# Turning the inputs of the second mixture by block transposes on VectorE and DMAs through DRAM instead of TensorE's transposes

## The chip, the cores and the metric

The kernel runs on one core of a Trainium2 chip. The metric is device microseconds of one execution. Engines are named as the profile names them: PE (TensorE, matrix products and transposes), PEld (its weight loads), DVE (VectorE), ACT (ScalarE), POOL (GpSimd) and SP (SyncE, which here issues every DMA).

## What is computed

Three stages follow each other: an attention with pooled queries, a first mixture with a gate, and a second mixture. The change is in the second one:

```python
def _moe2_ref(x, w_theta, w_tok_r, w_tok_i, w_ch):      # x: 4 x 576 x 512
    theta = x @ w_theta
    cos_t, sin_t = (np.cos(theta), np.sin(theta))
    zr = x * cos_t
    zi = x * sin_t
    y = einsum('ts,bsd->btd', w_tok_r, zr) + einsum('ts,bsd->btd', w_tok_i, zi)
    u = x + y
    return u + np.maximum(u @ w_ch, 0.0)
```

All of it is float32. The kernel computes each product as three products of float32r halves (`PASS`), a high and a low part of both operands.

## The kernel before

The first mixture leaves x transposed: `XT[b]` holds, for batch b, the 512 features on 4 x 128 partitions and the 576 tokens along the columns. The second mixture needs x both ways. `theta(n)` takes features on partitions (a block of 128 tokens of `XT` as the stationary operand); the products `x * cos` and `x * sin` need the same 128 tokens on partitions, because theta comes out of TensorE that way.

There are 18 blocks, `angles`: five for the even batches (four of 128 tokens and one that holds the last 64 tokens of two batches), four for the odd ones. For each block n:

- `turn(n)` makes the token-major copy: four TensorE transposes into PSUM bank 6 (L1042), and two ScalarE copies (L1045) into the tiles `yt[n, 0]` and `yt[n, 1]`, whose tags are t0 and t1 for even n, t2 and t3 for odd n.
- `ysplit(n)` cuts the feature-major block into its high and low part (ScalarE, and POOL at L1033).
- `theta(n)` makes twelve products (L1084), then VectorE reduces the angle (`near`, L1090 to L1092; `rest`, L1095 and L1096; `clip`, L1099), ScalarE makes sine and cosine (`wave`), and `mult` multiplies them by `yt` (L1114: the first on VectorE, the second on POOL; for the shared blocks `tails`, L1074 and L1075), and `zcut` cuts the result in two (L1065, L1066).

`mix(b, c0)` then mixes the tokens (L1138): nine parts of twelve products, one part for each piece of the token weights `WTK[j]`. `final(b, c0)` makes the product with `w_ch` (L1157) and stores the output.

What sets the order is a count of ticks. Each part of a product of TensorE ends with `tick()`; `after(k, f)` puts f k ticks ahead. `theta(n)` ends with `prepare(n + 1)`, which puts `turn(n + 1)` at TURN ticks and `ysplit(n + 1)` at YS ticks; `rest`, `clip`, `wave` and `mult` come at 1, 2, 4 and 5 ticks (`THETA`). Each engine works through its own list in the order in which it was written.

Around the seam of the two mixtures the order is hidden(6), theta(0), value(6), theta(1), hidden(7), theta(2), the first half of value(7), theta(3), the rest of value(7), theta(4), mix(0, 0). `hidden` (L841) and `value` (L860) are products of the first mixture. Between theta(4) and mix(0, 0) stand the DMA loads of the token weights: nine of 576 KB (L1180), into the buffers of value(7)'s weights, so that all but the first wait for a part of value(7); behind them four loads of w_ch (L1183).

Of the kernel before, what the change touches and what calls it, by code (L numbers as in the profile page):

```python
# [11 lines left out]
F32 = mybir.dt.float32  # L12
# [3 lines left out]
ALU = mybir.AluOpType  # L16
# [12 lines left out]
HALF = 288  # L29
# [1 line left out]
THIRDS = 6  # L31
AHEAD = 3
SHIFT = 24
TURN = 4
TPOS = ((1, 0), (1, 3), (2, 0), (3, 0), (3, 3))
THETA = (1, 2, 4, 5)
YM = (1, 0)
# [25 lines left out]
def attn_moe_kernel(ctx: ExitStack, tc: tile.TileContext, qT, kT, vP, muk, mur, wk, wv, wr, wth, wtr, wti, wch, ident, out):  # L63
    nc = tc.nc
    pe, act, dve, pool, sp = nc.tensor, nc.scalar, nc.vector, nc.gpsimd, nc.sync
# [3 lines left out]
    dram = ctx.enter_context(tc.tile_pool(name="dram", bufs=2, space=DRAM))  # L69

    idn = const.tile([128, 128], F32, name="idn")
# [9 lines left out]
    XT = [big.tile([128, 4, 577 + 63 * (1 - b % 2)], F32, name=f"xt{b}") for b in range(NB)]  # L81
# [630 lines left out]
    def mixtures(WR, nat, cp):  # L712
# [4 lines left out]
        def mem_tile(shape, dt, tag):  # L717
            return (early if tag in EARLY_TAGS else mem).tile(shape, dt, tag=tag, name=tag)
# [9 lines left out]
        def psum_at(i):  # L728
            return (psm + psn)[i]()
# [9 lines left out]
        def tile_x(i):  # L739
            return mem_tile([128, 576], F32R, f"x{i}")  # L740

        def tile_g(i):
            return mem_tile([128, 1152], F32, f"g{i}")
# [8 lines left out]
        def tile_q(i):  # L752
            return mem_tile([128, 1024], F32R, f"q{i}")

        def pair(t):
            return t.rearrange("p (a b) -> p a b", a=2)
# [5 lines left out]
        def after(n, fn, *args):  # L762
            queue.setdefault(now[0] + n, []).append((fn, args))

        def tick():
            now[0] += 1
            for fn, args in queue.pop(now[0], []):
                fn(*args)
# [116 lines left out]
        for k in range(4):  # L885
            x = pair(ready[k // 2][:, 576 * (k % 2):576 * (k % 2) + 576])
# [33 lines left out]
        t = now[0] + 1.0  # L920
# [116 lines left out]
        def turn(n):  # L1037

            b, i = angles[n]
            ps = psum_at(6)  # L1040
            for k in range(4):
                pe.transpose(ps[:, 128 * k:128 * k + 128], XT[b][:, k, 128 * i:128 * i + 128], idn)  # L1042
            for a in range(2):
                yt[n, a] = mem_tile([128, HALF], F32, f"t{2 * (n % 2) + a}")
                act.copy(yt[n, a][:, 0:256], ps[:, 256 * a:256 * a + 256])  # L1045

        yt = {}

        def prepare(n):
            if n < len(angles):  # L1050
                after(TURN, turn, n)
                if n:
                    after(YS, ysplit, n)
# [3 lines left out]
        def zcut(j, z):  # L1057
            assert cnt.get(j, 2) == 2
            cnt[j] = 0
            if j == 9:  # L1060
                zs[j] = [tile_x(4 - Y0 + a)[:, 0:DM] for a in range(2)]
            else:
                t = tile_a(zroom[j])
                zs[j] = [t[:, 0:DM], t[:, DM:2 * DM]]
            act.copy(zs[j][0], z)  # L1065
            pool.tensor_tensor(zs[j][1], z, zs[j][0].bitcast(F32), ALU.subtract)  # L1066

        def tails(yn, q, r):
            for o in range(2):
                z = tile_x(6 - Y0 + o)[:, 0:DM].bitcast(F32)  # L1070
                c = slice(64 * o, 64 * o + 64)
                for a, y in enumerate(yn):
                    w = slice(256 * a, 256 * a + 256)
                    dve.tensor_tensor(z[0:64, w], y[c, 0:256], q[c, w], ALU.mult)  # L1074
                    dve.tensor_tensor(z[64:128, w], y[c, 0:256], r[c, w], ALU.mult)  # L1075
                zcut(8 + o, z)

        def theta(n):
            b, i = angles[n]
            y = ys.pop(n)  # L1080
            ps = psum_at(4)
            for k in range(4):
                for p, (x, w) in enumerate(PASS):
                    pe.matmul(ps, lhsT=y[k // 2][:, k % 2, x], rhs=WT[k][:, w], start=(k == 0 and p == 0), stop=(k == 3 and p == 2))  # L1084
            tick()
            qr = tile_q(n % 2).bitcast(F32)
            q, r = qr[:, 0:DM], qr[:, DM:2 * DM]

            def near():
                dve.tensor_scalar(q, ps, float(np.float32(1 / (2 * math.pi))), MAGIC, op0=ALU.mult, op1=ALU.add)  # L1090
                dve.tensor_scalar(q, q, -MAGIC, 1.0, op0=ALU.add, op1=ALU.mult)
                dve.scalar_tensor_tensor(out=r, in0=q, scalar=-C1, in1=ps, op0=ALU.mult, op1=ALU.add)  # L1092

            def rest():
                dve.scalar_tensor_tensor(out=r, in0=q, scalar=-C2, in1=r, op0=ALU.mult, op1=ALU.add)  # L1095
                dve.scalar_tensor_tensor(out=r, in0=q, scalar=-C3, in1=r, op0=ALU.mult, op1=ALU.add)  # L1096

            def clip():
                dve.tensor_scalar(r, r, PI_LO, -PI_LO, op0=ALU.min, op1=ALU.max)  # L1099

            def wave():
                act.activation(q, r, AF.Abs)  # L1102
                act.activation(r, r, AF.Sin)
                act.activation(q, q, AF.Sin, scale=-1.0, bias=hpi)

            def mult():
                yn = [yt.pop((n, a)) for a in range(2)]
                if i == 4:
                    tails(yn, q, r)
                    return  # L1110
                for j, t in ((i, q), (4 + i, r)):
                    for a in range(2):
                        w = slice(256 * a, 256 * a + 256)
                        (dve, pool)[YM[j // 4]].tensor_tensor(t[:, w], yn[a][:, 0:256], t[:, w], ALU.mult)  # L1114
                    zcut(j, t)

            near()
            for t, f in zip(THETA, (rest, clip, wave, mult)):
                if t:
                    after(t, f)  # L1120
                else:
                    f()
            prepare(n + 1)
            tick()
# [59 lines left out]
        n = 5  # L1184
# [61 lines left out]
```

## Time and profile before

| | us |
|---|---|
| median of 3 runs | 917.83 |
| lowest and highest | 917.63, 918.45 |
| the profiled execution | 917.41 |
| span of the profiled execution | 915.6 |
| its second mixture, first L1042 to the end | 643.9 to 915.6 |

The span is the time from the first to the last instruction that the profile shows; the time of an execution is 1.8 us longer here. The second mixture shares its start with the last two blocks of the first one. The rows of the trace on which the prediction rests stand in a section of their own below; a row of a timeline gives the start, the length, the engine, the line, the operation with its tiles (out <- in), a count of merged instructions, and in brackets the idle time ahead of it and what ended that.

### The profile page before, as it was taken

To read this page: it belongs to the slowest core of one execution; us is meant where nothing else is said; L and a number is where in the kernel's file an instruction comes from. 1 tells how busy PE (TensorE), PEld (TensorE's weight loads), DVE (VectorE), ACT (ScalarE), POOL (GpSimd) and SP (SyncE) were. 2 spreads that over 40 slices of the span, in tenths; PEclk is the share of its full clock that TensorE was granted. 3 is DMA by queue.
4 is the path that set the end of the run, shared out by engine and by line. 5 is a ranking of instruction groups with operands and counts; after the bars stand their busy time and mean duration, and the time that the engine had idled before them with its cause. 6 is when DMAs were issued, how large, how long until landed. Compare 5 with 4: busy or idle time off the path is not lost.

```text
span 915.6 us, 17370 instructions
## 1 busy us (share of the span) xinstructions
PE 902.5 (99%) x6292; PEld 783.0 (86%) x6292; DVE 689.0 (75%) x965; ACT 540.2 (59%) x1131; POOL 594.8 (65%) x660
## 2 busy tenths in 40 slices
PE   8999999999999999999899999999999999999998
PEld 6777777777777777777889999999999999999998
DVE  7988888888988888882689888888758563676712
ACT  7777777777777777764665655555354442443410
POOL 7877777777787777764386566656567574665631
PEclk9999999999999999999999999999999999999999
DMA  7567877776777886659503333333508000010001
GB/s 225 170 183 218 241 222 191 214 216 206 216 209 211 241 229 188 176 154 346 224 12 116 100 99 104 96 98 113 187 2 273 27 28 26 1 53 1 27 26 52
DMA packets 59157, 130.92 MB, mean 143 GB/s; under 512 B 10816, under 2 KB 29952, under 8 KB 59072
## 3 DMA queue, kind: packets, MB, share of 16 engines
q1 hardware_dynamic: 59072, 129.82, 47.6%
q8 instruction: 49, 0.80, 0.4%
q14 instruction: 36, 0.29, 0.1%
HBM read 70.46 MB, written 22.17 MB: 101 GB/s over the span
## 4 chain that ended last, share of the span: by engine, by line
PE 91%; POOL 3%; DMA 2%; ACT 1%; issue 1%; DVE 1%; SPq 0%; ACTq 0%; DVEq 0%; POOLq 0%
PE sc L310 18%; PE ty L430 16%; PE ps L1138 13%; PE ps L860 11%; PE ps L841 10%; PE ps L1157 6%; PE ps L1084 5%; PE ty L396 4%; PE ps L810 3%; PE tx L396 3%; DMA b<-wv 2%; PE sc L396 2%; PE ps L1042 1%; POOL q L201 1%; POOL kt L201 1%
## 5 line engine op out<-in xcount | busy, mean ns | idle before, releaser
L331 DVE TENSOR_REDUCE m<-sc 128x1 f32<-128x1152 f32 x138 | 185.8, 1347 | 46.3 <-PE sc L310 45.6
L343 ACT ACTIVATE e<-sc,m 128x1152 f32<-128x1152 f32 x144 | 176.4, 1225 | 60.9 <-DVE m L331 56.3
L310 PE MATMUL sc<-kt,q 128*128 128x384 f32 (+1 forms) x864 | 192.1, 351 | 1.6 <-ACT E L407 1.0
L310 PEld LDWEIGHTS sc<-kt,q 128*128 128x128 f32 (+1 forms) x864 | 146.8, 190 | 22.4 <-issue 13.8
L1138 PE MATMUL ps<-b,a 128*128 128x288 f32 x816 | 111.2, 295 | 0.0
L1138 PEld LDWEIGHTS ps<-b,a 128*128 128x128 f32 x816 | 109.3, 188 | 0.6
L841 PE MATMUL ps<-x,a 128*128 128x288 f32 x768 | 105.3, 298 | 2.5 <-ACT g L823 2.4
L841 PEld LDWEIGHTS ps<-x,a 128*128 128x128 f32 x768 | 103.8, 191 | 3.0 <-ACT g L823 2.6
L860 PE MATMUL ps<-k,b 128*128 128x288 f32 x768 | 103.5, 295 | 0.0
L860 PEld LDWEIGHTS ps<-k,b 128*128 128x128 f32 x768 | 102.1, 188 | 0.3
L201 POOL TENSOR_TENSOR kt<-kn,kh 64x576 fp32r<-64x576 f32 (+1 forms) x64 | 87.5, 1387 | 2.4
L363 DVE STREAM_TRANSPOSE blk<-e 128x1152 f32<-128x1152 f32 x60 | 81.6, 1360 | 7.5 <-ACT e L343 7.5
L430 PE MATMUL ty<-M,vn 128*64 128x320 f32 x576 | 84.4, 438 | 0.2 <-ACT M L407 0.2
L430 PEld LDWEIGHTS ty<-M,vn 128*64 128x64 f32 x576 | 38.7, 136 | 36.3 <-issue 3.8
L476 POOL TENSOR_TENSOR xt<-xt,rb 128x576 f32<-128x576 f32 x16 | 21.9, 1370 | 73.0 <-ACT xt L440 73.0
L828 POOL TENSOR_TENSOR k<-h,k 128x288 fp32r<-128x288 f32 x64 | 59.1, 939 | 15.1 <-ACT k L827 14.9
L430 PE MATMUL ty<-E,vn 128*64 128x256 f32 x540 | 64.9, 385 | 0.0
L844 DVE TENSOR_TENSOR h<-h 128x288 f32<-128x288 f32 x64 | 42.3, 663 | 22.3 <-ACT h L843 21.6
L1102 ACT ACTIVATE q<-q 128x512 f32<-128x512 f32 x18 | 11.4, 632 | 77.2 <-DVE q L1099 77.2
L810 PE MATMUL ps<-x,blk 128*128 128x288 f32 x384 | 54.3, 301 | 2.1 <-POOL x L790 1.9
L407 DVE COPY M<-tx 128x512 f32<-128x512 f32 x80 | 54.5, 681 | 1.8 <-PE tx L396 1.8
L430 PEld LDWEIGHTS ty<-E,vn 128*64 128x64 f32 x540 | 36.1, 136 | 22.8 <-issue 7.6
(147 smaller groups left out, 1753.3 us busy)
## 6 DMA issues: line engine op xcount, KB each, us to landing
E<-blk SPq DMA_DIRECT2D x240, 144.0 KB
vn<-vP SPq DMA_DIRECT2D x16, 576.0 KB
kn<-kT SPq DMA_DIRECT2D x15, 576.0 KB
qn<-qT SPq DMA_DIRECT2D x15, 576.0 KB
b<-wtk SPq DMA_DIRECT2D x9, 576.0 KB
rb<-scr SPq DMA_DIRECT2D x32, 144.0 KB
out<-xt SPq DMA_DIRECT2D x32, 144.0 KB
cv<-wk SPq DMA_DIRECT2D x8, 512.0 KB
```

What stands on the lines that cost most here:

```text
L201: engines[e].tensor_tensor(out, x, hi.bitcast(F32), ALU.subtract)
L310: r = pe.matmul(sc[0:m, c, 0:384], lhsT=x, rhs=k[:, 384 * c:384 * c + 384], start=(i == 0), stop=(i == len(ops) - 1),)
L331: r = dve.tensor_reduce(m, scs[n][:, :, 0:384], axis=AX.XY, op=ALU.max, negate=True)
L343: r = act.activation(e, sc[:, :, 0:384], AF.Exp, bias=m, scale=1.0, accum_out=rss[P][:, t:t + 1])
L363: dve.transpose(out, es_[n].rearrange("p a b -> p (a b)").rearrange("p (k m i) -> p k m i", k=KT, m=4))
L396: r = pe.transpose(ps[:, 128 * j:128 * j + 128], flat[:, 128 * k:128 * k + 128], idn)
L430: pe.matmul(out, lhsT=vns[P][:, h, j], rhs=e, start=(x == 0), stop=(x == KT - 1))
L810: pe.matmul(pss[d], lhsT=WR[k][:, w, 128 * d:128 * d + 128], rhs=x[k][:, c], start=(k == 0 and n == 0), stop=(k == 3 and n == 2))
L828: pool.tensor_tensor(q[:, 1], h, q[:, 0].bitcast(F32), ALU.subtract)
L841: pe.matmul(ps, lhsT=WK[k, f // 4][:, w, 128 * (f % 4):128 * (f % 4) + 128], rhs=x[k][:, c], start=(k == 0 and n == 0), stop=(k == 3 and n ...
L860: pe.matmul(pss[d], lhsT=WV[f][:, w, 128 * d:128 * d + 128], rhs=k2[f][:, c], start=(f == 0 and n == 0), stop=(f == 7 and n == 2))
L1138: pe.matmul(pss[d], lhsT=zs[j][z][:, 128 * d:128 * d + 128], rhs=WTK[min(j, 8)][:, w, cs], start=(m == 0 and n == 0), stop=(m == 8 and n = ...
```

## The change

`turn(n)` no longer uses TensorE. VectorE transposes the block in 32 x 32 pieces, in two instructions of 256 columns each; each result is written by a DMA to a DRAM tile `turned`; eight DMAs read it back, 32 partitions each, so that all four groups of 32 tokens reach their partitions. The columns of `yt` are then in another order (groups of 32 features by quarter), and `mult` and `tails` walk the angle tiles in that order. TURN becomes 2. The room for the transposed blocks is tile g1 for the first five blocks, then the tiles h0 to h2.

```diff
-TURN = 4
+TURN = 2
         def turn(n):
             b, i = angles[n]
-            ps = psum_at(6)
-            for k in range(4):
-                pe.transpose(ps[:, 128 * k:128 * k + 128], XT[b][:, k, 128 * i:128 * i + 128], idn)
+            d = dram.tile([128, 4, 128], F32, tag="turned", name="turned")
+            if n < 5:
+                if not spares:
+                    spares.append(tile_g(1))
+                rooms = [spares[0][:, 512 * (n % 2) + 256 * u:512 * (n % 2) + 256 * u + 256] for u in range(2)]
+            else:
+                rooms = [mem_tile([128, HALF], F32, f"h{(2 * n + u) % 3}")[:, 0:256] for u in range(2)]
+            for u, t in enumerate(rooms):
+                src = XT[b][:, :, 128 * i + 64 * u:128 * i + 64 * u + 64].rearrange("p k (m j) -> p k m j", m=2)
+                dve.transpose(t.rearrange("p (m k j) -> p k m j", m=2, k=4), src)
+                sp.dma_start(out=d[:, 2 * u:2 * u + 2], in_=t.rearrange("p (m x) -> p m x", m=2))
             for a in range(2):
-                yt[n, a] = mem_tile([128, HALF], F32, f"t{2 * (n % 2) + a}")
-                act.copy(yt[n, a][:, 0:256], ps[:, 256 * a:256 * a + 256])
+                t = yt[n, a] = mem_tile([128, HALF], F32, f"t{2 * (n % 2) + a}")
+                for m in range(4):
+                    sp.dma_start(out=t[32 * m:32 * m + 32, 0:256].rearrange("j (q x) -> j q x", q=2), in_=d.rearrange("(q j) m x -> j q m x", q=4)[:, 2 * a:2 * a + 2, m])
+        spares = []
+        def by_quarter(t, a):
+            return t.rearrange("p (k q j) -> p q k j", k=4, q=4)[:, 2 * a:2 * a + 2]
+        def turned_half(t):
+            return t.rearrange("p (q k j) -> p q k j", q=2, k=4)
...
-                    w = slice(256 * a, 256 * a + 256)
-                    dve.tensor_tensor(z[0:64, w], y[c, 0:256], q[c, w], ALU.mult)
-                    dve.tensor_tensor(z[64:128, w], y[c, 0:256], r[c, w], ALU.mult)
+                    for d, t in ((slice(0, 64), q), (slice(64, 128), r)):
+                        dve.tensor_tensor(by_quarter(z[d], a), turned_half(y[c, 0:256]), by_quarter(t[c], a), ALU.mult)
...
-                        w = slice(256 * a, 256 * a + 256)
-                        (dve, pool)[YM[j // 4]].tensor_tensor(t[:, w], yn[a][:, 0:256], t[:, w], ALU.mult)
+                        w = by_quarter(t, a)
+                        (dve, pool)[YM[j // 4]].tensor_tensor(w, turned_half(yn[a][:, 0:256]), w, ALU.mult)
```

SP's list ahead of mix(0, 0) before: the last stores of the converted w_ch, then the loads of the token weights (b8, b0, ... are the buffers, wtk0, wtk4, ... the pieces; in brackets the semaphores that the row waits for, a DMAHW one being that of an earlier DMA):

```order
L153 DMA wch3_4586<-a12_7487 128x256 [waits DMAHW5_49,DMAHW0_49,Activation_49]
L154 DMA wch3_4586<-a12_7487 128x256 [waits Pool_49]
L1180 DMA b8_8190<-wtk0_4574 128x1152 [waits DMAHW4_49,DMAHW3_49,DVE_49]
L1180 DMA b0_8191<-wtk4_4578 128x1152 [waits PE_49]
L1180 DMA b1_8192<-wtk1_4575 128x1152 [waits DMAHW1_49,PE_49]
```

And in the changed kernel, where L1050 are the two writes of turn(4), L1054 its reads, and L1196 the same loads of the token weights:

```order
L1050 DMA turned_8127<-g1_7465 128x256 [waits DMAHW7_49,DVE_49]
L1050 DMA turned_8127<-g1_7465 128x256 [waits DMAHW0_49,DVE_49]
L1054 DMA t0_8132<-turned_8127 32x2x128 [waits DMAHW7_49,DMAHW1_49,Pool_49]
L1054 DMA t0_8132<-turned_8127 32x2x128 [waits DMAHW2_49]
L1054 DMA t0_8132<-turned_8127 32x2x128 [waits DMAHW3_49,DMAHW0_49]
L1054 DMA t0_8132<-turned_8127 32x2x128 [waits DMAHW4_49]
L1054 DMA t1_8137<-turned_8127 32x2x128 [waits DMAHW5_49,Pool_49]
L1054 DMA t1_8137<-turned_8127 32x2x128 [waits DMAHW6_49]
L1054 DMA t1_8137<-turned_8127 32x2x128 x2
L1196 DMA b8_8221<-wtk0_4574 128x1152 [waits DMAHW1_49]
L1196 DMA b0_8222<-wtk4_4578 128x1152 [waits DMAHW2_49,PE_49]
```

Between the stores of w_ch and the token weights now stand the ten DMAs of each of turn(1) to turn(4), the last of them directly ahead of the loads.

DVE's list around theta(3) before, from the second multiplication of theta(2) (q_7983) over the six steps of theta(3) (q_8083):

```order
L1114 TENSOR_TENSOR q_7983<-t_7860,q_7983 128x256
L1090 TENSOR_SCALAR q_8083<-ps 128x512
L1091 TENSOR_SCALAR q_8083<-q_8083 128x512
L1092 SCALAR_TENSOR_TENSOR q_8083<-q_8083,ps 128x512
L1095 SCALAR_TENSOR_TENSOR q_8083<-q_8083 128x512
L1096 SCALAR_TENSOR_TENSOR q_8083<-q_8083 128x512
L1099 TENSOR_SCALAR q_8083<-q_8083 128x512
L866 TENSOR_TENSOR xt_72<-ps,sg 128x288 x4
```

And in the changed kernel, where theta(2) works in q_8002 and theta(3) in q_8108:

```order
L1049 STREAM_TRANSPOSE g_7465<-xt_69 128x4x2x32 x2
L1130 TENSOR_TENSOR q_8002<-t_7824,q_8002 128x2x4x32
L1130 TENSOR_TENSOR q_8002<-t_7829,q_8002 128x2x4x32
L1106 TENSOR_SCALAR q_8108<-ps 128x512
L1107 TENSOR_SCALAR q_8108<-q_8108 128x512
L1108 SCALAR_TENSOR_TENSOR q_8108<-q_8108,ps 128x512
L1111 SCALAR_TENSOR_TENSOR q_8108<-q_8108 128x512
L1112 SCALAR_TENSOR_TENSOR q_8108<-q_8108 128x512
L1115 TENSOR_SCALAR q_8108<-q_8108 128x512
L1049 STREAM_TRANSPOSE g_7465<-xt_69 128x4x2x32 x2
L866 TENSOR_TENSOR xt_72<-ps,sg 128x288 x4
```

The pair of transposes of turn(3) stands ahead of theta(2)'s multiplications, that of turn(4) behind theta(3)'s clip.

## Rows read from the trace of the kernel before

**Rows 1.** The page: busy time of the engines, and the chain by engine.

```profile
PE 902.5 (99%) x6292; PEld 783.0 (86%) x6292; DVE 689.0 (75%) x965; ACT 540.2 (59%) x1131; POOL 594.8 (65%) x660
PE 91%; POOL 3%; DMA 2%; ACT 1%; issue 1%; DVE 1%; SPq 0%; ACTq 0%; DVEq 0%; POOLq 0%
```

**Rows 2.** Chain in order of time, 640 to 916: start us, us, what.

```profile
644.09 0.44 PE ps L1042 x4
...
695.23 4.76 PE ps L860 x36
...
704.80 4.76 PE ps L1138 x36
...
710.00 9.48 PE ps L1138 x72
719.48 2.79 PE ps L1084 x12
...
859.75 0.44 PE ps L1042 x4
```

**Rows 3.** Groups, 640 to 916: busy us, mean ns, idle before and its releasers.

```profile
L1114 POOL TENSOR_TENSOR q<-t,q 128x256 f32<-128x256 f32 x32 | 24.5, 785 | 47.7 <-ACT q L1104 47.7
...
L1114 DVE TENSOR_TENSOR q<-t,q 128x256 f32<-128x256 f32 x32 | 14.4, 490 | 12.9 <-ACT q L1103 12.9
...
L1045 ACT COPY t<-ps 128x256 f32<-128x256 f32 x36 | 11.2, 362 | 0.0
```

**Rows 4.** Busy by stretch: length; PE, PEld, DVE, ACT, POOL; PEclk, DMA, GB/s.

```profile
640.00:916.00 276.00, 272.26 (x1903) 262.25 (x1902) 158.93 (x259) 101.43 (x231) 149.09 (x156) 1.00 0.17 58
```

**Rows 5.** VectorE's block transposes: ns min/median/max, first and last start, forms.

```profile
L455 DVE STREAM_TRANSPOSE rt<-r x16: 211/211/213, 38.4 to 420.1; 128x32 f32<-128x32 f32 x16
...
L363 DVE STREAM_TRANSPOSE blk<-e x60: 1334/1364/1379, 33.1 to 399.8; 128x1152 f32<-128x1152 f32 x60
```

**Rows 6.** Timeline of DVE around theta(3), and theta(5): start us, us, what.

```profile
694.43 0.76 DVE L1114 TENSOR_TENSOR q<-t,q 128x256 f32<-128x256 f32 x2 [1.37 <-ACT q L1103]
695.27 0.69 DVE L1090 TENSOR_SCALAR q<-ps 128x512 f32<-128x512 f32 x1
...
700.83 0.85 DVE L1099 TENSOR_SCALAR q<-q 128x512 f32<-128x512 f32 x1
...
722.38 0.69 DVE L1090 TENSOR_SCALAR q<-ps 128x512 f32<-128x512 f32 x1 [2.40 <-PE ps L1084]
...
726.22 0.43 DVE L1099 TENSOR_SCALAR q<-q 128x512 f32<-128x512 f32 x1
```

**Rows 7.** Timeline of SP: DMAs issued, start us and us.

```profile
42.70 10.09 SPq L372 DMA_DIRECT2D E<-blk  x16
...
630.58 0.32 SPq L154 DMA_DIRECT2D wch<-a  x1
632.35 0.33 SPq L122 DMA_DIRECT2D a<-wch  x1
...
660.66 41.71 SPq L1180 DMA_DIRECT2D b<-wtk  x9
```

**Rows 8.** DMAs from DRAM into 64 partitions by line: ns of issue min/median/max.

```profile
L470 SPq DMA_DIRECT2D rb<-scr x32: 482/586/696, 41.5 to 424.6; - x32
```

**Rows 9.** Busy time by stretch, columns as in rows 4, around the large loads.

```profile
664.00:666.00 2.00, 2.00 (x17) 2.00 (x16) 0.00 (x0) 1.97 (x3) 0.00 (x0) 1.00 0.00 0
...
698.00:700.00 2.00, 2.00 (x17) 2.00 (x17) 1.97 (x2) 0.31 (x2) 2.00 (x2) 1.00 0.97 293
...
702.00:704.00 2.00, 2.00 (x11) 1.60 (x10) 1.80 (x6) 1.97 (x5) 0.58 (x2) 1.00 0.93 270
...
708.00:710.00 2.00, 2.00 (x18) 2.00 (x18) 1.97 (x2) 0.00 (x0) 2.00 (x3) 1.00 1.03 414
```

**Rows 10.** The same view where TensorE paused between the attention and the mixture.

```profile
445.00:448.00 3.00, 0.59 (x5) 0.43 (x4) 3.00 (x7) 3.00 (x10) 0.95 (x2) 1.00 0.94 345
449.00:453.00 4.00, 3.91 (x18) 3.71 (x17) 1.96 (x4) 1.89 (x5) 1.19 (x1) 0.57 0.02 5
```

## The prediction

> **What bounds the kernel now.** I read the page's busy shares and chain first, then the chain in order of time over the second mixture, then the timelines of VectorE and SyncE around the one place where the chain could turn. TensorE is busy 99% of the span and makes 91% of the chain [rows 1]. From 640 us to the end the chain is TensorE piece after piece [rows 2]: whatever leaves TensorE there shortens the run, until another engine or a DMA ends last. The page's average says nothing on how near the others are; [rows 6, 7] do, and they show two close neighbours. VectorE runs without a gap from the multiplication of theta(2) into theta(3) (694.43 + 0.76 = 695.19, next start 695.27), so it is behind TensorE there and not waiting for it. And SyncE's nine loads of the token weights begin at 660.66 and are drawn out over 41.71 us; the first mix that reads them starts at 704.80.
>
> **What is removed.** 18 turns of four transposes each are pieces of 0.43 or 0.44 us in the chain, the first at 644.09, the last at 859.75 [rows 2]. 18 x 0.437 = 7.9 us leave TensorE, all of it on the path. The 36 copies of ScalarE (362 ns each, 11.2 us [rows 3]) lie beside the path and are worth nothing here. Were nothing late, the run would take 917.4 - 7.9 = 909.5 by the profiled execution.
>
> **What is added on VectorE.** Per turn two block transposes of 256 columns. Rows exist for 32 columns (211 ns) and 1152 (1364 ns) [rows 5]; a straight line between them gives 211 + 224 x 1.03 = 442 ns, which I take; the two rows themselves are the bounds. That is 0.9 us a turn, 16 us in all, on an engine that is busy 158.93 of the last 276 us [rows 4]. The multiplications now walk q in runs of 32 numbers. No row shows that walk; the transposes of [rows 5] walk in runs of 32 at about one number a nanosecond, so I keep the present 490 ns on VectorE and 785 ns on POOL [rows 3], with twice as much as upper bound and nothing below, since the number of elements stays.
>
> **What is added on SyncE, and what is queued behind it.** Ten DMAs a turn: two writes of 128 KB that wait for the transposes, and eight reads of 32 KB into 32 partitions each, of which the first waits for a write to land. Per DMA the issue row of a store to DRAM is 0.32 (L154 in [rows 7]). The reads fill 32 partitions; the nearest rows are 16 copies into 32 partitions issued in 10.09 us, so 0.63 each [rows 7], and loads from DRAM into 64 partitions at 0.586 [rows 8]. I take 0.6, so 4.8 us for eight, and keep 0.36 (store-like, with a gap) to 0.65 as ends. The moving itself (32 KB at some 290 GB/s [rows 9]) is 0.11 us.
>
> The Trainium skill, page "DMA: Bandwidth & Descriptors", section "Issuing engines are not separate DMA queues", says that the issuing time is "usually small relative to the DMA itself"; for small reads [rows 7, 8] say the opposite. By the rule the reads would cost their moving alone, and the time would be that of the first rival, 918.1.
>
> In most of the stage this queue time is hidden: a turn is issued at least 8 ticks of 1.6 us before its multiplication, some 13 us, against 0.9 + 1.8 + 4.8 + 3.3 = 10.8 us from transposes to data (the terms stand below; the last is that of a load eighteen times a read's size). Behind turn(0) on SyncE stands the last raw load of w_ch, which slips by up to the 4.8 us of its eight reads, and behind that the conversion on VectorE ahead of theta(0). The cover is the time until hidden(7) needs value(6)'s banks; I price it at 0 to 1 us and take 0.
>
> The cover fails at one place. The order shows all ten DMAs of turn(4) ahead of the nine token weight loads, and turn(4)'s transposes behind clip(3) on VectorE. Step by step:
>
> - clip(3) ends at 700.83 + 0.85 = 701.7 [rows 6]. That TensorE is earlier by four turns does not move it, since VectorE is the late one; the transposes of turn(3) fit in the 1.37 us for which mult(2) waits [rows 6]. So 701.7 stays. At the earliest it is the end of theta(3) on TensorE plus a quick chain: 695.23 [rows 2] less four turns is 693.5, and 722.38 to 726.65 is 4.3 [rows 6], so 697.8. At the latest it slips by two pairs of transposes, 703.4.
> - The first transpose ends at 702.2, its write is issued then, and lands 1.8 us after (store at 630.58, the load that waits for it at 632.35 [rows 7]): 704.0.
> - Eight reads of 0.6: 708.8. Now the first token weight load is issued. Before, the load at 660.66 had all landed by 664, when the DMA share is zero [rows 7, 9], so 3.3 us: 712.1.
>
> TensorE would come to mix(0, 0) at 704.80 - 5 x 0.437 = 702.6. It stalls until 712.1, which is 7.3 us later than now.
>
> Then the mix runs at the loads' pace. A part of it takes 9.48 / 6 = 1.58 us [rows 2]. A load is 0.59 MB; where the engines are full these loads move 293 GB/s, and rows of 4 KB 414 [rows 9]. I take 310, 1.90 us a load, as the late loads no longer wait for TensorE one by one; ends 270 (2.2 us) and 400 (1.5 us). The last of the nine lands 8 x 1.90 = 15.2 us after the first, at 727.3, and the mix ends at 728.9; now it ends at 719.48. So +9.4 us at this point. If the loads are quicker than TensorE, the clock is the floor: after a stretch with TensorE busy 0.59 of 3 us the granted clock over the 4 us from 449 was 0.57, part of them at 1.2 instead of 2.4 GHz, which cost 4 x 0.43 = 1.7 us [rows 10]; the mix then takes 14.3 + 1.7 = 16.0 instead of 16.8, so the floor is 0.8 below my value.
>
> After it 12 of the 18 turns are still to be saved, 12 x 0.437 = 5.2. **Sum: +9.4 - 5.2 = +4.2 us.** The four loads of w_ch come 9 us later too, but final(0, 0) is two mixes away. The profiled execution took 917.41, so 921.6; the median of the three runs is 0.42 above that execution, so **922.0**.
>
> **The rivals.** *Cheap reads.* If a read costs the store's 0.36, the loads start 1.9 us earlier; if it costs its moving alone, 4.8 - 8 x 0.11 = 3.9: 920.1 and 918.1. For it: they are plain copies of 512-byte runs. Against it: both rows that fill fewer than 128 partitions [rows 7, 8]. With the mix at the clock's floor as well, 0.8 less, this lands within 0.2%, about 918.3.
>
> *VectorE catches up (faster).* If VectorE reaches clip(3) when TensorE allows, at 697.8, the loads start 3.9 us earlier; with reads at 0.36 it is 5.8, with the mix at the clock's floor 6.6, and the sum is -2.4: 915.4. It decides from the point where mult(2) no longer ends after theta(3). For it: ScalarE has lost its copies and answers sooner. Against it: the gapless rows [rows 6] and 0.9 us more work a turn. The whole -7.9 is out of reach as long as the loads stand behind turn(4).
>
> *Slow walks.* If the regrouped multiplications take twice as long, mult(0) to mult(2) add 3 x 0.98 us on VectorE ahead of clip(3), and POOL's (785 ns, then 1.6) hold turn(4)'s first read, which waits for POOL to release its tile: +2 to +4 on the loads, and later thetas wait on POOL as well. 925 to 930. It decides from a doubling on.
>
> **How the numbers follow.** Forecast 0.62 (slower by 0.3 to 0.9%), cheap reads 0.17 (no change), VectorE catches up 0.11 (faster), slow walks 0.10. Measurement tells 0.2%, 1.8 us. So faster 0.11, same 0.17, slower 0.72. The range: below, cheap reads with part of the other rival, 916.6; above, 0.65 a read (+0.4), two pairs of transposes (+1.7), loads at 270 GB/s (+2.3), and a microsecond for turn(0), 927.4.
>
> **What would show it.** Right: no L1042 on TensorE; a TensorE pause of 7 to 10 us ahead of the first mix, ended by a token weight load, and a granted clock of 0.50 in or behind it; SyncE busy with turn(4)'s reads until some 709; reads near 0.6 us each; no other pause above 1 us after 730. Wrong: a first mix at about 703, which would say that the loads were not held; reads at 0.3 us; pauses in the later mixes, where theta then waits for turned data or POOL, which would make the loss larger and of another kind.

## The result, and the profile after

The changed kernel takes 924.68 us (median; 924.28 to 926.13) against 917.73 us (917.05 to 918.66) for the kernel before: a ratio of 1.0077, with a 95% interval of 1.0067 to 1.0088. It is slower by 0.8%. The profiled execution took 924.28 us, its span is 922.5 us.

Line numbers have moved: the transposes are L1049, their writes L1050, the reads L1054; near is L1106 to L1108, rest L1111 and L1112, clip L1115, the multiplications L1130, theta L1100, the mix L1154, final L1173, the token weight loads L1196.

Busy time on the page, which answers to [rows 1]:

```profile
PE 897.4 (97%) x6220; PEld 776.7 (84%) x6220; DVE 700.3 (76%) x1001; ACT 530.4 (57%) x1095; POOL 596.3 (65%) x660
```

TensorE has 72 instructions and 5.1 us less to do, and the run is longer: it waits. Where it waits, in the second mixture (us in total, times, longest):

```profile
PE ps L1154 <- DMA b<-wtk: 7.5, 1, 7.5
PE ps L1100 <- DVE q L1108: 1.5, 1, 1.5
PE ps L1100 <- POOL x L1033: 0.7, 1, 0.7
PE ps L860 <- ACT h L843: 0.5, 1, 0.5
```

Before, this view has no row for the second mixture. There is one large pause, ahead of the first part of mix(0, 0), and it ends with a token weight load. The chain over the same place, which answers to [rows 2] (start us, us, what):

```profile
704.75 0.46 DVE g L1049 x2
705.21 1.72 DMA turned<-g
...
707.00 0.32 SPq L1054
...
710.67 3.98 DMA b<-wtk
...
714.70 17.16 PE ps L1154 x108
```

It no longer runs through TensorE there, but through turn(4): its transposes, the landing of its write, the issue of its reads by SyncE, and only then the first token weight load. SyncE's timeline and VectorE's, which answer to [rows 7] and [rows 6] (L122 loads the raw w_ch, L1016 the theta weights):

```profile
641.48 2.03 SPq L1016 DMA_DIRECT2D blk<-wth  x4
...
644.72 1.79 SPq L1050 DMA_DIRECT2D turned<-g  x2
651.85 3.62 SPq L1054 DMA_DIRECT2D t<-turned  x8
655.51 0.42 SPq L122 DMA_DIRECT2D a<-wch  x1
...
705.21 0.81 SPq L1050 DMA_DIRECT2D turned<-g  x2
707.00 3.62 SPq L1054 DMA_DIRECT2D t<-turned  x8
710.67 4.89 SPq L1196 DMA_DIRECT2D b<-wtk  x9
```

```profile
662.08 0.68 DVE L1106 TENSOR_SCALAR q<-ps 128x512 f32<-128x512 f32 x1
...
697.56 0.76 DVE L1130 TENSOR_TENSOR q<-t,q 128x256 f32<-128x256 f32 x2 [0.68 <-ACT q L1119]
698.24 0.68 DVE L1106 TENSOR_SCALAR q<-ps 128x512 f32<-128x512 f32 x1
...
704.00 0.83 DVE L1115 TENSOR_SCALAR q<-q 128x512 f32<-128x512 f32 x1
```

VectorE again has no gap from the multiplication of theta(2) into theta(3), and there it is 3.0 to 3.2 us later than in [rows 6]. SyncE's timeline shows where that may begin: the last raw load of w_ch, L122, is issued at 655.51 behind turn(0)'s eight reads. In the kernel before, the load and the first step of theta(0) on VectorE stand at:

```profile
652.15 0.33 SPq L122 DMA_DIRECT2D a<-wch  x1
```

```profile
658.76 0.68 DVE L1090 TENSOR_SCALAR q<-ps 128x512 f32<-128x512 f32 x1
```

So the load is 3.4 us later and theta(0)'s first step 3.3. The load reaches VectorE by way of ScalarE, whose first step of the conversion waits for it, 5.6 us instead of 2.9:

```profile
ACT a L126 <- DMA a<-wch: 5.6, 1, 5.6
```

The eight reads are late themselves: turn(0)'s writes, issued from 644.72 behind the four 512 KB loads of L1016, have landed only at 651.85; turn(4)'s take from 705.21 to 707.00.

The mix itself takes 17.16 us; before, three pieces from 704.80 to 719.48 less a turn [rows 2], 14.24. By stretch (columns as in [rows 4]: length; PE, PEld, DVE, ACT, POOL; PEclk, DMA, GB/s):

```profile
707.00:710.00 3.00, 0.20 (x1) 0.00 (x0) 2.90 (x6) 1.25 (x3) 2.27 (x3) 1.00 0.18 50
710.00:711.00 1.00, 0.00 (x0) 0.00 (x0) 1.00 (x1) 0.51 (x2) 1.00 (x2) 0.70 0.26 71
711.00:714.00 3.00, 0.00 (x0) 0.00 (x0) 2.93 (x5) 0.49 (x1) 3.00 (x3) 0.50 0.77 208
714.00:721.00 7.00, 6.30 (x27) 6.31 (x28) 4.49 (x9) 2.61 (x5) 2.31 (x4) 0.53 1.02 416
721.00:732.00 11.00, 11.00 (x85) 10.96 (x84) 1.29 (x4) 0.80 (x3) 1.21 (x2) 1.00 0.96 381
```

The granted clock falls from 1.00 to 0.50 (from 2.4 to 1.2 GHz) while TensorE stands still, and comes back some 6 us after it has begun again. The loads move 416 GB/s, so one of 0.59 MB takes 1.42 us.

**Where the time went.** The mix ends at 731.86 instead of 719.48: +12.4. Six turns less on TensorE give -2.6 (five ahead of the mix, one in it); the four pauses cost 10.2, the longer mix 2.9; 1.9 us are left that the listed waits don't hold. Half of that was there before the first of the four pauses: theta(0) begins 0.5 us later in this execution, at 651.26 against 650.75, with a turn of 0.44 less ahead of it. Behind the mix no pause follows, and the other twelve turns are saved: 12.4 - 5.2 = 7.2, and the span is 6.9 longer.

### The profile page after: what moved, and what is told of

Same layout as the page of the kernel before. It is cut to its first block, busy times and chain, and to the rows that moved or that the text cites. A ratio compares the mean times of both kernels' runs of the same rounds, so it can differ in the third digit from the quotient of the medians.

```text
span 922.5 us, 17589 instructions
## 1 busy us (share of the span) xinstructions
PE 897.4 (97%) x6220; PEld 776.7 (84%) x6220; DVE 700.3 (76%) x1001; ACT 530.4 (57%) x1095; POOL 596.3 (65%) x660
## 5 line engine op out<-in xcount | busy, mean ns | idle before, releaser
L1154 PE MATMUL ps<-b,a 128*128 128x288 f32 x816 | 112.7, 299 | 7.5 <-DMA b<-wtk 7.5
L1154 PEld LDWEIGHTS ps<-b,a 128*128 128x128 f32 x816 | 111.7, 193 | 8.5 <-DMA b<-wtk 7.9
L841 PE MATMUL ps<-x,a 128*128 128x288 f32 x768 | 103.3, 295 | 2.5 <-ACT g L823 2.4
L810 PEld LDWEIGHTS ps<-x,blk 128*128 128x128 f32 x384 | 52.9, 193 | 4.7 <-POOL x L790 2.9
L790 POOL TENSOR_TENSOR x<-t,x 128x288 fp32r<-128x288 f32 x52 | 44.7, 877 | 17.0 <-ACT x L789 16.8
```

What stands on the lines that cost most here:

```text
L810: pe.matmul(pss[d], lhsT=WR[k][:, w, 128 * d:128 * d + 128], rhs=x[k][:, c], start=(k == 0 and n == 0), stop=(k == 3 and n == 2))
L841: pe.matmul(ps, lhsT=WK[k, f // 4][:, w, 128 * (f % 4):128 * (f % 4) + 128], rhs=x[k][:, c], start=(k == 0 and n == 0), stop=(k == 3 and n ...
L1154: pe.matmul(pss[d], lhsT=zs[j][z][:, 128 * d:128 * d + 128], rhs=WTK[min(j, 8)][:, w, cs], start=(m == 0 and n == 0), stop=(m == 8 and n = ...
```

## The experiments

The theory after this: the loss is made at one place, by what SyncE has to issue ahead of the token weight loads, and by what follows from that pause; everywhere else the change is a gain. The rivals: the new way costs a little at every turn; VectorE's additional work is the cause; the loads, and not the clock, pace the first mix. In kernels with both ways of turning, theta is L1113, the mix L1171, the new writes and reads are L1058 and L1062, the loads L1213.

| run | what is different | us, median | ratio to the kernel before, 95% |
|---|---|---|---|
| 1 | only turns 0 to 4 new | 931.01 | 1.0123 to 1.0159 |
| 2 | only turns 5 to 17 new | 912.64 | 0.9925 to 0.9960 |
| 3 | all new, turn(0) behind the w_ch load | 920.75 | 1.0026 to 1.0046 |
| 4 | all new but turn(4) | 916.50 | 0.9975 to 0.9994 |
| 5 | changed kernel, 60 transposes ahead of the mix, 44 more products at its start | 929.68 | 1.0123 to 1.0163 |
| 6 | four writes and two reads a turn | 925.36 | 1.0074 to 1.0104 |
| 7 | turn(4) behind the token weight loads | 923.16 | 1.0045 to 1.0075 |
| 8 | all new but turn(3), turn(4); turn(0) behind the w_ch load | 910.26 | 0.9908 to 0.9937 |
| 9 | changed kernel, 60 transposes ahead of the mix | 923.85 | 1.0052 to 1.0086 |
| 10 | run 8 with turn(3) new | 911.17 | 0.9915 to 0.9944 |
| 11 | run 8 with turn(0) ahead of the w_ch load | 915.99 | 0.9971 to 0.9990 |
| 12 | the changed kernel again | 925.25 | 1.0057 to 1.0092 |

**Runs 1 and 2: the change in halves.** Both kernels hold both ways of turning, and `OLD` lists the turns that stay on TensorE, with their multiplications as before: turns 5 to 17 in run 1 (the diff), turns 0 to 4 in run 2.

```diff
-TURN = 2
+TURN = 2; OLD = range(5, 18)
...
             b, i = angles[n]
+            if n in OLD:
+                ps = psum_at(6)
+                for k in range(4):
+                    pe.transpose(ps[:, 128 * k:128 * k + 128], XT[b][:, k, 128 * i:128 * i + 128], idn)
+                for a in range(2):
+                    yt[n, a] = mem_tile([128, HALF], F32, f"t{2 * (n % 2) + a}")
+                    act.copy(yt[n, a][:, 0:256], ps[:, 256 * a:256 * a + 256])
+                return
...
-                after(TURN, turn, n)
+                after(4 if n in OLD else TURN, turn, n)
```

> Turns 0 to 4 go the new way, turns 5 to 17 stay on TensorE. Theory: the whole loss is made at the seam by the first five turns (token weight loads held behind turn(4)'s DMAs, then a low clock), and the thirteen later turns are pure gain. Then this kernel keeps the loss and gives back 13 x 0.437 = 5.7 us of the gain: 924.7 + 5.7 = 930.4 us, with the pause of some 7.5 us ahead of the first mix as in the changed kernel. Rival: the added DMAs and VectorE work lose time all along, so that the 14.9 us (7.0 lost plus 7.9 removed) spread evenly over 18 turns: 5 x 0.39 = 1.9 us over the kernel before, 919.7.

> Turns 0 to 4 stay on TensorE, turns 5 to 17 go the new way. Theory (the loss is made at the seam alone): the seam is that of the kernel before, no pause ahead of the first mix, and 13 x 0.437 = 5.7 us leave TensorE: 917.7 - 5.7 = 912.0 us. Rival (the loss is spread over all turns): 13 x 0.39 = 5.1 us over the kernel before, 922.8.

Measured: 931.01 and 912.64, both within 0.7 us of the theory and 10 us from the rival. Run 1 has the pause of 7.5 us ahead of the mix; in run 2 the view of waits has no row at all for the second mixture, and the chain is TensorE throughout:

```profile
705.01 14.24 PE ps L1171 x108
```

So thirteen new turns gain 4.7 us, and the first five cost 13.7 us.

**Run 3: turn(0) behind the load that it holds.**

```diff
-                after(TURN, turn, n)
+                after(TURN if n else 4, turn, n)
```

> All turns go the new way; only turn(0) is put two ticks later, so that its ten DMAs stand behind the last raw load of w_ch on SyncE and not ahead of it. The work is the same. Theory: turn(0)'s DMAs ahead of that load are what moved VectorE's chain from theta(0) to clip(3) 3.1 us later; the load is issued at 652 again instead of 655.5, clip(3) ends near 701.7, the first token weight load is issued near 707.6, and the time falls by 3.1 us to 921.6. Rival: the chain is late because VectorE has more to do (the transposes, 0.83 us a turn); then the load moves and clip(3) does not, and the time stays at 924.7.

Measured: 920.75, 3.9 us less than the changed kernel, with the same work on every engine. On SyncE:

```profile
653.30 0.33 SPq L122 DMA_DIRECT2D a<-wch  x1
...
708.64 4.72 SPq L1196 DMA_DIRECT2D b<-wtk  x9
```

And clip(3) on VectorE:

```profile
701.96 0.83 DVE L1115 TENSOR_SCALAR q<-q 128x512 f32<-128x512 f32 x1
```

clip(3) ends at 702.8 instead of 704.8, and the first token weight load goes out at 708.64 instead of 710.67: 2.0 us earlier in the two traces, where the theory had 3.1. So the order alone of turn(0)'s ten DMAs and one load moves clip(3), and against the rival, by which clip(3) stays, the theory holds. But 1.1 us of the lateness against the kernel before (701.7) remain. theta(0) begins 0.6 us later in this execution; how much of the rest is VectorE's 0.83 us a turn isn't shown. The profiled execution took 921.81 us, 1.1 more than the median.

**Run 4: turn(4) alone on TensorE** (`OLD` is 4).

> turn(4) alone stays on TensorE, the other seventeen go the new way, so that the token weight loads stand behind turn(3)'s reads (ended at 702.9 in the changed kernel) instead of turn(4)'s (710.7). Theory: the loads' place behind turn(4) on SyncE is the cause of the pause. First load issued near 702.9, first product of the mix 4.0 later at 706.9, TensorE ready at 707.2 + 0.44 because VectorE is still late: pause under 0.5 us, the clock stays at 1.00, the mix takes 14.3 us and ends near 722.0 instead of 731.9: 914.8 us. Rival 1: loads issued together with eight more to come pace the mix at 1.9 us each, so that it ends near 724 with pauses at its parts: 917. Rival 2: the pause comes from VectorE's lateness, of which this edit takes 0.83 us only: 924.

Measured: 916.50, 8.2 us less than the changed kernel. No wait for a load is left, and the mix takes 14.24 us again (chain):

```profile
708.89 14.24 PE ps L1171 x108
```

The mix begins at 708.89 and not at the theory's 707.6, and the time is 1.7 us above its 914.8. What it lacked lies further ahead, in value(7), where TensorE now waits 2.4 us (in the changed kernel's trace 0.5) and then works at half the clock:

```profile
PE ps L860 <- ACT h L843: 2.4, 1, 2.4
```

```profile
689.00:692.00 3.00, 3.00 (x14) 3.00 (x15) 1.86 (x2) 1.27 (x4) 2.92 (x4) 0.51 0.00 0
692.00:693.00 1.00, 1.00 (x7) 1.00 (x7) 0.84 (x2) 0.65 (x2) 1.00 (x2) 0.77 0.00 0
```

Three us at 0.51 and one at 0.77 are 1.7 us of lost clock.

**Runs 5 and 9: clock or loads.** TensorE is kept busy through the pause with transposes whose results nobody reads:

```diff
+        ps = psum_at(6)
+        for k in range(60):
+            pe.transpose(ps[:, 128 * (k % 4):128 * (k % 4) + 128], XT[0][:, k % 4, 0:128], idn)
```

> The changed kernel with 60 more transposes on TensorE between theta(4) and mix(0, 0), into the PSUM bank 6 that nobody uses any more; their results are not used. At 0.109 us each they fill 6.5 of the 7.5 us for which TensorE pauses there. Theory: the first mix takes 17.16 us instead of 14.24 because of the granted clock of 0.50 until 721, not because of the loads (410 GB/s, 1.43 us a load against 1.58 us a part). With TensorE busy through the pause the clock stays at 1.00, the mix again takes 14.3 us and the time falls by 2.8 us to 921.9. Rival: the loads pace the mix; then it still takes 17 us, the time stays at 924.7, and TensorE shows pauses at the mix's parts that end with a token weight load.

In run 5 the number 60 also went to the products with which the kernel starts, so its time says nothing on the question; only its trace does. Run 9 has the edit alone.

> As the fifth run, but only with the 60 transposes ahead of the first mix: there the change had also raised the number of products with which the kernel starts from 16 to 60, which moved everything by some 7 us. Its trace showed the first mix at 14.84 us with the granted clock at 1.00, against 17.16. Theory (the clock makes the difference): 924.7 - 2.3 = 922.4 us. Rival (the loads pace the mix, or the transposes only shift the loss): 924.7.

Measured: 923.85, so 0.8 us less and not 2.3; between the two. The trace of run 9 at the mix:

```profile
709.00:715.00 6.00, 6.00 (x58) 6.00 (x57) 5.83 (x7) 1.75 (x4) 5.26 (x6) 1.00 0.39 97
...
717.00:722.00 5.00, 5.00 (x40) 5.00 (x40) 4.36 (x8) 1.08 (x3) 1.31 (x1) 1.00 1.03 420
```

```profile
716.33 15.15 PE L1154 MATMUL ps<-b,a 128*128 128x288 f32 x108 [0.86 <-DMA b<-wtk]
```

```profile
722.93 1.63 PEld L1154 LDWEIGHTS ps<-b,a 128*128 128x128 f32 x12 [0.22 <-DMA b<-wtk]
724.89 6.35 PEld L1154 LDWEIGHTS ps<-b,a 128*128 128x128 f32 x48 [0.34 <-DMA b<-wtk]
```

(The second fence is TensorE's timeline, the third that of its weight loads.) The clock stays at 1.00 and the mix takes 15.15 us. So of the 2.9 us by which the mix was longer, 2.0 are the clock's, and 0.9 stay with that gone. Of these TensorE's weight loads show 0.6 as waits for token weights, in the middle of the mix; the rest is not assigned. Both theories hold a part.

It is the trace that says so, and not the time: the ratios of the two kernels, 1.0052 to 1.0086 and 1.0067 to 1.0088, overlap. Nor does the span show the 2.0, because the whole seam came later in this execution:

```profile
712.41 4.71 SPq L1196 DMA_DIRECT2D b<-wtk  x9
```

That is 1.7 us behind the 710.67 of the changed kernel's trace. The last raw load of w_ch was issued 0.9 us later, at 656.44, and TensorE waited 2.4 us in value(7), where the changed kernel's trace has 0.5.

**Run 12: is that 0.5 us the rule?**

> The changed kernel once more, nothing altered. In its profiled execution TensorE waits 0.5 us in value(7) for ScalarE; five of the kernels above that are the same up to there wait 1.5 to 2.4 us, and two of them show a granted clock of 0.50 for some microseconds behind that. If the 0.5 is the exception, this profile shows some 2 us there, TensorE comes to the first mix later and waits less for the first load, and the time stays at 924.7 within 0.2%; the gain of the ninth run (0.8 us in the median against 2.0 in the first mix of its trace) is then cut down by that pause. If the changed kernel always waits 0.5, the profile repeats it, and something else cut the gain.

Measured: 925.25, with executions from 923.55 to 927.73. The profiled one waits 2.4 us in value(7) and then 7.4 us for the load:

```profile
PE ps L1154 <- DMA b<-wtk: 7.4, 1, 7.4
PE ps L860 <- ACT h L843: 2.4, 1, 2.4
```

```profile
714.51 4.51 SPq L1196 DMA_DIRECT2D b<-wtk  x9
```

So the 0.5 us is not the rule; but the pause ahead of the mix did not shrink for the longer wait, and this execution took 927.73. The last raw load of w_ch was issued at 658.56 in it, 3.0 us later than in the first profile of the same kernel, and the first token weight load 3.8 us later; the time is 3.4 us longer. How late the w_ch load is differs between executions of one kernel, and the held loads move with it. By how much this cut the gain of run 9 can't be said from one profile each; that stays open.

**Run 6: fewer, larger reads.**

```diff
-                sp.dma_start(out=d[:, 2 * u:2 * u + 2], in_=t.rearrange("p (m x) -> p m x", m=2))
+                for m in range(2):
+                    sp.dma_start(out=d.rearrange("(m j) q x -> m q j x", m=4)[2 * u + m], in_=t[:, 128 * m:128 * m + 128])
...
-                for m in range(4):
-                    sp.dma_start(out=t[32 * m:32 * m + 32, 0:256].rearrange("j (q x) -> j q x", q=2), in_=d.rearrange("(q j) m x -> j q m x", q=4)[:, 2 * a:2 * a + 2, m])
+                sp.dma_start(out=t[:, 0:256], in_=d[:, 2 * a:2 * a + 2])
```

> Four writes and two reads a turn instead of two writes and eight reads; the DRAM tile gets the tokens along its rows, the bytes moved are the same. Theory: a DMA costs SyncE 0.35 to 0.45 us to issue, whatever its size between 32 and 128 KB. Behind the last transpose then stand two writes (0.8), the landing (1.8) and two reads (0.9): turn(4) holds the token weight loads until some 708.0 instead of 710.7, and turn(0) lets the last raw load of w_ch go 2.7 us sooner as well. Both together: 924.7 - 2.7 - 2.3 = 919.7 us; if only turn(4)'s part counts, 922.0. Rival: the time goes with the bytes or the rows, so that the two larger reads take as long as the eight (3.6 us): 924.7.

Measured: 925.36, no change; the theory's gain did not come. SyncE at turn(4):

```profile
705.41 2.21 SPq L1051 DMA_DIRECT2D turned<-g  x4
710.38 0.81 SPq L1054 DMA_DIRECT2D t<-turned  x2
711.23 4.84 SPq L1196 DMA_DIRECT2D b<-wtk  x9
```

The reads are as the theory has them: 0.40 us each with the gaps for 128 KB, no more than for 32 KB. But the writes, now in pieces of 512 bytes that go to places with three strides, take 0.55 each, and the first read starts 5.0 us after the first write instead of 1.8. From the first write to the first load it is 5.82 us; in the changed kernel 710.67 - 705.21 = 5.46. What was saved on the reads went into the writes and their landing. Which of the two properties of the writes does it was not tried.

**Run 7: turn(4) behind the loads.**

```diff
-                after(TURN, turn, n)
+                if n != 4:
+                    after(TURN, turn, n)
...
             sp.dma_start(out=WTK[j].bitcast(F32), in_=WD["wtk", j])
+        turn(4)
```

> turn(4) is called behind the nine token weight loads; all turns go the new way. The loads are issued from 702.9, behind turn(3)'s reads, the first product of the mix is at 706.9, TensorE has no pause there and the clock stays at 1.00. What is open is turn(4) itself: its data is needed by the last part of mix(0, 0), due at 707.2 + 12.7 = 719.9. If its writes are moved beside the loads, they are issued at 707.6 and land at 710.2, the reads end at 713.8, their data is there at 715.8, VectorE's eight short multiplications take 3.5 us and the cut some 2: a pause of 1 to 2 us, 916. If the writes move only when the 5.3 MB issued ahead of them have moved (12.9 us at 412 GB/s), they land at 718, the data is there at 724 and the last part starts at 729: a pause of 9 us, a low clock behind it, and 926.

Measured: 923.16, between the two cases and near the second. The pause has moved to the last part of the mix, which waits 5.0 us for turn(4)'s data. SyncE:

```profile
703.79 4.49 SPq L1197 DMA_DIRECT2D b<-wtk  x9
713.80 0.80 SPq L1050 DMA_DIRECT2D turned<-g  x2
719.63 4.11 SPq L1054 DMA_DIRECT2D t<-turned  x8
```

The writes were ready later than I had put them (VectorE came to the transposes at 713.3), but what was asked is answered: a write that lands in 1.8 us elsewhere takes 5.8 us when the loads are in front of it, until 719.6; the nine loads, begun at 703.8, need 12.8 us at 416 GB/s. The Trainium skill, page "DMA: Bandwidth & Descriptors", section "Two DMAs through the same engine are not ordered", says that within one queue of one DMA engine descriptors start in order. The times of this trace agree with that: the write lands behind the time that the loads need. They do not exclude that the write moved beside the loads and was slowed by them.

**Runs 8, 10 and 11: what is left of the price.** Run 8 keeps turn(3) and turn(4) on TensorE and puts turn(0) behind the w_ch load; run 10 makes turn(3) new as well (`OLD` is 4 alone); run 11 puts turn(0) back (without `or n == 0`).

```diff
-TURN = 2
+TURN = 2; OLD = (3, 4)
...
-                after(TURN, turn, n)
+                after(4 if n in OLD or n == 0 else TURN, turn, n)
```

> turn(3) and turn(4) stay on TensorE and turn(0) stands behind the last raw load of w_ch; sixteen turns go the new way. Theory: now nothing holds the token weight loads, and what is left of the new way's price ahead of the first mix is VectorE's 0.83 us a turn. Against the kernel with turns 0 to 4 on TensorE (912.6) three more turns leave TensorE, 1.3 us, if VectorE's lateness (0.5 + 0.7 us of TensorE's pauses with all turns new) is gone: 911.3; if it is not, 912.5. Rival: some turn of the first three costs more than it saves even without a held load: above 914.

> Only turn(4) stays on TensorE, turn(0) stands behind the last raw load of w_ch: the eighth run with turn(3) the new way as well. If turn(3) costs nothing, one turn more leaves TensorE: 910.3 - 0.4 = 909.8 us. Theory: turn(3)'s reads again hold the token weight loads until about 699.7 (by the trace of the third run, shifted to the start of this one's second mixture), the first product of the mix comes 4.0 to 4.4 later, at 703.9 against 703.3 in the eighth run, and the time is 910.9 us. Rival: VectorE's two transposes more push theta(4) back by over a microsecond: 911.5 or more.

> The eighth run with turn(0) back ahead of the last raw load of w_ch: the price of that place alone, now that no held load hides it. Theory: VectorE's chain from theta(0) on is 3.3 us later, and TensorE waits for it at hidden(7) and theta(3) for 2.4 + 0.5 + 0.3 us, as in the fourth run: 910.3 + 3.2 = 913.5 us. The prediction's price, 0 to 1 us: 910.3 to 911.3.

Measured: 910.26, 911.17, 915.99. Run 8 is 7.2 us faster than the kernel before it was timed with (917.49), against 16 x 0.44 = 7.0: sixteen turns at their full value, and no wait of TensorE in the second mixture. It beats both kernels. In run 10 turn(3)'s reads hold the loads until 699.73, as forecast (699.7), and the view of waits shows how close that is:

```profile
PE ps L1171 <- DMA b<-wtk: 0.2, 1, 0.2
```

Run 11 is 5.7 us slower than run 8 by the place of turn(0) alone; 3.2 was expected, and 0 to 1 in the prediction. Its waits are near the expected ones, 2.4 and 0.4, and behind the first the clock falls:

```profile
689.00:690.00 1.00, 1.00 (x6) 0.80 (x6) 1.00 (x2) 0.77 (x3) 1.00 (x2) 0.88 0.24 97
690.00:693.00 3.00, 3.00 (x14) 3.00 (x14) 1.70 (x3) 1.29 (x5) 2.92 (x4) 0.50 0.55 177
693.00:694.00 1.00, 1.00 (x9) 1.00 (x9) 1.00 (x2) 0.45 (x2) 1.00 (x2) 0.91 0.15 60
```

That is 1.7 us; 2.8 + 1.7 = 4.5 of the 5.7, and the rest is not assigned.

## Why the prediction was right

The forecast, 922.0 and slower by 0.3 to 0.9%, named the mechanism that the trace and runs 1, 2 and 4 show: token weight loads held behind turn(4), one pause, and no other after it. Its terms, one by one:

- **The gain of a turn** (0.437 us, all on the path): right. Run 8 measures 0.45 a turn; run 2 gives 0.36.
- **Transposes at 0.442 us, multiplications as before**: right. A transpose takes 0.416, a regrouped multiplication 0.419 on VectorE and 0.741 on POOL in the median. Slow walks fell with that.
- **The landing of a write, 1.8 us**: right for turn(4) (705.21 to 707.00). turn(0)'s, behind the loads of the theta weights, took 7.1 us from the first issue (644.72 to 651.85).
- **A read, 0.6 us**: too high. Eight take 3.62, 0.45 each: -1.1 us with the gaps. Cheap reads in the sense of the rival (their moving alone) did not come. The rule of the Trainium skill that issuing is usually short beside the DMA itself (page "DMA: Bandwidth & Descriptors", section "Issuing engines are not separate DMA queues") does not hold for reads this small: 0.45 us to issue, against 0.08 us for 32 KB at 416 GB/s.
- **turn(0)'s place ahead of the w_ch load, 0 to 1 us, taken at 0**: this is the step that failed. The load slipped by 3.4 us, within the 4.8 that the prediction allowed, but the slip was not covered: by run 3 the place costs 3.9 us in the time, and by run 11 5.7. clip(3) ends at 704.8 instead of 701.7, beyond the prediction's latest, 703.4; of these 3.1 us run 3's trace gives 2.0 back, and the other 1.1 are not shown to be turn(0)'s. The reads went out as late as they did because turn(0)'s write landed late, a delay that the prediction had not priced. The cover that it named, the time until hidden(7) needs value(6)'s banks, is TensorE's; but the held load feeds VectorE by way of ScalarE, and [rows 6] showed VectorE without a gap from theta(2)'s multiplication into theta(3).
- **From the first load's issue to the mix, 3.3 us**: 4.0. That the loads start at 710.67 and not at 708.8 is the sum of these: +3.1 for clip(3), -0.1 for the transpose, -1.1 for the reads. That the reads were priced too high hid a third of what clip(3) was late, and that is luck.
- **TensorE ready at 702.6**: the prediction left TensorE undisturbed until the mix. It waits 2.7 us on the way and loses the 1.9 that are left above, and would have been ready at 707.2. Under the held loads this cost nothing; where the loads come free it is what is left (run 4).
- **The mix paced by the loads at 1.90 us each**: the wrong one of two. The loads move 416 GB/s, the higher row of [rows 9], not the mean that was taken; the pace is set in the main by the clock, which was kept as a floor. 16.8 us were forecast and 17.16 measured, so the size was right for another reason, by luck. Run 9 shows both: 2.0 us go with the clock, and 0.9 stay without it, of which 0.6 are waits for loads.

Too low by 2.7 us in all: the first product of the mix came at 714.70 instead of 712.1, and the rest of the sum, 0.4 for the mix, was near. *VectorE catches up* fell by the same row that spoke against it: VectorE got later, not earlier.

## What to carry to other kernels

A DMA that waits for an engine's result costs its queue the time of the wait and of its issue, and whatever is written behind it starts later; look for what stands behind it, and for which engine the held transfer feeds. If that engine has no gap ahead of the place that matters, do not take the delay as covered. Replace work on the busiest engine only where the replacement's latency is covered: here sixteen of eighteen turns, in another order, give 0.8%, and all eighteen lose as much.

## What the runs showed of the hardware

- SyncE takes 0.42 us (median of 144) to issue a read of 32 KB into 32 partitions and 0.35 (median of 36, run 6) to issue one of 128 KB into 128: no more for four times the bytes. A write of 128 KB in rows of 1 KB takes 0.34 (median of 26); half of that in pieces of 512 bytes takes 0.52 (median of 52, run 6).
- A write of 128 KB landed 1.8 us after its issue where nothing large stood ahead of it in the queue (turn(4) of the changed kernel), 5.8 us behind nine loads of 576 KB (run 7), and turn(0)'s pair 7.1 us after the first issue, behind four loads of 512 KB (changed kernel).
- A pause of 2.4 us of TensorE was followed by a granted clock of 0.50 in runs 4, 9 and 11, and in run 12, at the same place and after as long a pause, the clock stayed at 1.00. A pause of 2.1 us there was followed by 0.50 in run 1, one of 2.2 us by 1.00 in run 7. In runs 4 and 11 the low clock cost 1.7 us.
